# Threshold attention followed by a leaky-ReLU layer pair: head 2 masked on ScalarE in every step, turn copies moved to VectorE, and a rearranged start

## The chip, the cores and the metric

The kernel runs on one core of a Trainium2 chip. The metric is device time in microseconds (us), the median of several executions. The core has a matrix engine (TensorE, PE in the profile; PEld are its weight loads), a vector engine (VectorE, DVE), a scalar engine (ScalarE, ACT), GpSimd (POOL), and SyncE (SP), which here only issues transfers (DMAs).

## The reference

Eight batches, eight heads, 576 tokens, head size 64. The attention keeps only scores within `tau` = 0.02 of the row's maximum. Its output, with the heads side by side, is the input of two dense layers.

```python
scores = scale * np.matmul(q, k.transpose(0, 1, 3, 2))
thresh = np.max(scores, axis=-1, keepdims=True) - tau
scores = np.where(scores >= thresh, scores, -1000000000.0)
attn = np.exp(scores - np.max(scores, axis=-1, keepdims=True))
attn = attn / (np.sum(attn, axis=-1, keepdims=True) + 1e-09)
x = np.matmul(attn, v)            # then (B*S, H*D) = (4608, 512)
h = x @ w_in                      # 512 -> 2048
out = np.maximum(0.01 * h, h) @ w_out   # 2048 -> 512
```

## The kernel before, in words

**Steps.** The work is cut into 144 steps, 18 for each batch. A step handles 128 query rows of a pair of heads (head 1 and head 2 of the pair, `h` = 0 and 1 in the code) against all 576 keys; the last two steps of a batch (tail steps) take the last 64 tokens of two pairs each. Iteration `n` of the loop at the end of the function issues the scores of step `n` and the later stages of earlier steps. Every engine works through its own instructions strictly in the order in which this loop issues them; nothing reorders them.

**q and k** must be exact beyond fp16, so each fp32 block is split into a high and a low fp16 half, scaled by 64. For the first blocks this is done on ACT (high, L158) and DVE (low, L159) by `split_now`; for all others on POOL by `split_scale` (L138), `split_high` (L144) and `split_low` (L148). `turn` (L162) transposes both halves on PE (L177) into a PSUM tile `tp` and copies that to `qT` or `kT` (L188, for the tails L180). The `tp` tile shares a ring of two PSUM buffers (tag `h`) with `hp`, the result of layer 1. `turns_at` says in which iteration a block is turned: ten per batch, and those of the next batch fall on ten of its 18 iterations.

**Scores.** `scores` (L217) makes the three products high-high, low-high, high-low of both heads, 12 matmuls for a step, into two PSUM tiles (tag `sc`). `copy_min` (L225, DVE) scales and negates them into the SBUF tile `s` and yields the row minimum; it also frees the PSUM tiles for the next step. `threshold` (L232) adds `tau`; it runs on DVE for steps below 14 and on POOL from then on.

**Mask and exponential.** Two ways exist. In the plain way ACT computes `e = exp(min - s)` (L254) and DVE multiplies by the comparison with the threshold and sums (L264, `weights`). In the *steep* way, for head 2 only, ACT pushes everything beyond the threshold to a huge negative value with a Prelu of slope 1e20 (L250), which needs the threshold, and takes the exponential with its sum (L251). Head 1 always goes the plain way. A step is steep if its number is below 12, or if the iteration after it has no turn.

**Normalisation and product with v.** `recip` (L270, DVE) inverts the sums, `widen` (L273) writes them into the last block of the weights tile. That tile is then transposed. For `early` steps (below 8) PE transposes (L291) and ACT and DVE copy (L293, `turn_w_pe`); for the others `turn_w` is a DMA transpose on SP's queue (L281), and `widen` runs on POOL. `pv` (L304) multiplies with v, four iterations after the second step of a pair, three for early ones. `evacuate` (L326, L316 for tails, DVE) multiplies by the reciprocal and writes `x`.

**Layers.** `layer1` (L347) makes 16 matmuls per iteration into `hp`, and ACT applies the leaky ReLU (L349) into `g`. `layer2` (L360) makes eight matmuls per iteration into a single PSUM tile `o`; ACT copies it out (L366, `osb`) and SP stores it. After the last step the queues `l1q`, `l2q` and `stores` are drained in the same loop.

**The order at the start** is written out by hand: the first three blocks are split at once, turned, then pair 1's k block (`first[3]`) is split, then the loop begins. In iteration 0 pair 1's q block (`first[4]`) is split behind the first `copy_min` and ahead of `threshold`, and both blocks are turned at the end of that iteration.

```python
for st in steps:
    st.steep = st.n < 12 or not turns_at.get(st.n + 1)
```

Of the kernel before, what the change touches and what calls it, by code (L numbers as in the profile page):

```python
# [9 lines left out]
FP32 = mybir.dt.float32  # L10
# [4 lines left out]
PV_LAG = 4  # L15


class Group:


    def __init__(self, tokens, where):
        self.tokens = tokens
        self.where = where
        self.x = None
        self.g = None


class Step:


    def __init__(self, n, b, blk, p, c):
        self.n, self.b, self.blk, self.p, self.c = n, b, blk, p, c
        self.tail = blk == 2

        self.early = n < 8


@with_exitstack
def kernel(
# [10 lines left out]
    nc = tc.nc  # L50
# [9 lines left out]
    ps = ctx.enter_context(tc.tile_pool(name="ps", bufs=1, space=bass.MemoryType.PSUM))  # L60
# [3 lines left out]
    ident = sb.tile([128, 128], FP16, name="ident")  # L64
# [54 lines left out]
    def turned_of(b, which):  # L119
        if (b, which) not in turned:  # L120
            turned[b, which] = sb.tile([128, 2, NP, WIDE[which]], FP16, tag=f"{which}T", bufs=2, name=f"{which}T")
        return turned[b, which]

    def pair_of(b, p, which):
        return raws[b, p // 2, which][:, ds(2 * (p % 2), 2), :].rearrange("p h (t d) -> p h t d", d=64)

    def new_half():
        return sb.tile([128, 2, 4, 2, 64], FP16, tag="half", bufs=4, name="half")
# [12 lines left out]
    def split_high(key):  # L141
        n = 2 if key[1] == "t" else 4
        halves[key] = new_half()
        nc.gpsimd.tensor_copy(out=halves[key][:, 0, 0:n, :, :], in_=scaled[key][:, 0:n, :, :])  # L144
# [6 lines left out]
    def split_now(key):  # L151
        t = halves[key] = new_half()
        for i in range(2):
            if key[1] == "t":
                src, n = tails[key[0], key[2]][:, :, i, :], 2
            else:
                src, n = pair_of(*key)[:, i, :, :], 4
            nc.scalar.activation(out=t[:, 0, 0:n, i, :], in_=src, func=AF.Copy, bias=0.0, scale=64.0)  # L158
            nc.vector.scalar_tensor_tensor(out=t[:, 1, 0:n, i, :], in0=src, scalar=64.0, in1=t[:, 0, 0:n, i, :],  # L159
                                           op0=AX.mult, op1=AX.subtract)  # L160

    def turn(key, copy=None):  # L162
        copy = copy or nc.scalar.copy
        b, p, which = key
        dst, half = turned_of(b, which), halves.pop(key)
        n = 2 if p == "t" else 4
        c0 = 0 if which == "q" else 64
        if p == "t":
            c0 = MAIN if which == "q" else 0
            tp = ps.tile([128, 2, 2, 2, 64], FP16, tag="h", bufs=2, name="tp")  # L170
        else:
            tp = ps.tile([128, 2, 4, 128], FP16, tag="h", bufs=2, name="tp")
        for x in range(2):
            for t in range(n):
                for h in range(2):
                    o = tp[ds(64 * h, 64), x, :, t, :] if p == "t" else tp[ds(64 * h, 64), x, t, :]
                    nc.tensor.transpose(o, half[:, x, t, h, :], ident[:, :])  # L177
        if p == "t":
            for x in range(2):
                copy(out=dst[:, x, :, ds(c0, 64)], in_=tp[:, x, :, :, :].rearrange("d u s p -> d (u s) p"))  # L180
            if which == "k" and b:
                nc.gpsimd.tensor_copy(out=dst[:, :, :, 576:640], in_=dst[:, :, :, 0:64])
            elif which == "k":
                for x in range(2):
                    nc.vector.tensor_copy(out=dst[:, x, :, 576:640],
                                          in_=tp[:, x, :, :, :].rearrange("d u s p -> d (u s) p"))
        else:
            copy(out=dst[:, :, p, ds(c0, 512)], in_=tp[:, :, :, :].rearrange("d x t p -> d x (t p)"))  # L188
# [3 lines left out]
    steps = []  # L192
# [36 lines left out]
    def threshold(st):  # L229
        st.th = sb.tile([128, 2, 2], FP32, tag="th", bufs=3, name="th")  # L230
        eng = nc.vector if st.n < 14 else nc.gpsimd
        eng.tensor_scalar(out=st.th[:, :, 0], in0=st.mn[:, :, 0], scalar1=1.0, scalar2=tau_f, op0=AX.mult, op1=AX.add)  # L232
# [118 lines left out]
        if u == nu - 1:  # L351
            l2q.extend((g, m, r) for m in range(T // 128) for r in range(8))

    def layer2():
        g, m, r = l2q.pop(0)
        if r == 0:
            g.o = ps.tile([128, 512], FP32, tag="o", bufs=1, name="o")
        for j in (2 * r, 2 * r + 1):
            for u2 in range(2):
                nc.tensor.matmul(out=g.o[ds(64 * u2, 64), :], lhsT=g.g[:, j, ds(128 * m + 64 * u2, 64)],  # L360
                                 rhs=w_out16[:, j, :], start=(j == 0), stop=(j == 15), skip_group_check=True)
        if r == 7:
            nm = g.tokens // 128
            if m == 0:
                g.osb = sb.tile([128, nm, 512], FP32, tag=f"osb{nm}", bufs=2 if nm == 2 else 1, name="osb")
            nc.scalar.activation(out=g.osb[:, m, :], in_=g.o[:, :], func=AF.Copy, bias=0.0, scale=1.0)  # L366
            if m == nm - 1:
                stores.append(g)
# [13 lines left out]
    loads_at, turns_at, pool_at = {}, {}, {}  # L382

    def at(d, n, f):
        d.setdefault(n, []).append(f)

    def units(b):
        u = [(b, p, w_) for p in range(NP) for w_ in "kq"]
        return u[:2] + [(b, "t", "k")] + u[2:] + [(b, "t", "q")]

    for b in range(1, B):
        base = PERB * (b - 1)
        for i, (s, w_) in enumerate(((0, "k"), (0, "q"), (1, "k"), (1, "q"))):
            at(loads_at, base + ((-2, 0, 5, 7)[i] if b > 1 else (3, 4, 8, 9)[i]),
               lambda b=b, s=s, w_=w_: load_main(b, s, w_))
        for i, w_ in enumerate("kq"):
            at(loads_at, base + (2, 12)[i] + 4 * (b == 1), lambda b=b, w_=w_: load_tails(b, w_))
        for i, key in enumerate(units(b)):
            n_ = base + 4 + 18 * i // 10 if b > 1 else 9 + 3 * i // 2
            at(pool_at, n_ - 3, lambda key=key: split_scale(key))  # L400
            at(pool_at, n_ - 3, lambda key=key: split_high(key))
            at(pool_at, n_ - 2, lambda key=key: split_low(key))
            at(turns_at, n_, lambda key=key: turn(key))
    for b in range(B):
        base = PERB * (b - 1)
        if b:
# [46 lines left out]
    def split_pool(key):  # L453
        split_scale(key)
        split_high(key)
        split_low(key)

    first = units(0)
    for key in first[:3]:
        split_now(key)  # L460
    turn(first[0])
    turn(first[1], nc.vector.tensor_copy)
    turn(first[2])
    split_now(first[3])
    for key in first[5:7]:
        split_pool(key)
    for i in range(4):
# [1 line left out]
    for n_, key in zip((0, 1, 6), first[7:]):  # L469
        at(pool_at, n_, lambda key=key: split_pool(key))  # L470
    at(turns_at, 0, lambda: turn(first[3]))
    at(turns_at, 0, lambda: turn(first[4], nc.vector.tensor_copy))
    for n_, key in zip((1, 2, 3, 4, 8), first[5:]):
        at(turns_at, n_, lambda key=key: turn(key, nc.vector.tensor_copy if key[2] == "q" else None))

    N = len(steps)
    for st in steps:
        st.steep = st.n < 12 or not turns_at.get(st.n + 1)
    pv_at = {s.n + PV_LAG - s.early: s for s in steps if s.tail or s.c == 1}
    n = 0  # L480
    while n < N + PV_LAG + 2 or l1q or l2q or stores:
        for f in loads_at.get(n, []):
            f()
        if 1 <= n <= N:
            exps(steps[n - 1])
        if n < N:
            scores(steps[n])
            copy_min(steps[n])
        if n == 0:
            split_now(first[4])  # L490
        todo = pool_at.get(n, [])
        for f in todo[:1]:
            f()
        if n < N:
            threshold(steps[n])
        for f in todo[1:]:
            f()
        if 1 <= n <= N:
            last = steps[n - 1]
            weights(last)  # L500
            if last.early:
                recip(last.pair, last.c, 1)
                widen(last.pair, last.c, 1, nc.vector)
            elif last.tail or last.c == 1:
                recip(last.pair, 0, last.pair.n)
                widen(last.pair, 0, last.pair.n)
                turn_w(last.pair)
        while stores:
            store()
        if l1q and l1q[0][3] <= n:  # L510
            layer1()
        for f in turns_at.get(n, []):
            f()
        if 2 <= n < N + 2 and steps[n - 2].early:
            turn_w_pe(steps[n - 2].pair, steps[n - 2].c)
        for _ in range(2):
            if l2q:
                layer2()
        if n in pv_at:
            pv(pv_at[n])  # L520
            evacuate(pv_at[n], n)
        n += 1
# [33 lines left out]
```

## Time and profile before

| what | value |
|---|---|
| median of three runs | 517.52 us (516.12 to 518.38) |
| the profiled execution | 517.33 us |
| its span in the trace | 515.6 us |
| mean granted TensorE clock | 0.995 |
| POOL th (L232) waiting for DVE's minimum (L225), 50 to 480 us | 63.9 us, 70 times |
| ACT Prelu (L250) waiting for POOL's th, the same stretch | 3.2 us, 3 times |
| DVE weights (L264) | 210 instructions, mean 875 ns |
| ACT k and q copies (L188) | 60 instructions, 1008 ns |
| DVE q copies (L188) | 4 instructions, 688 ns |

The page names groups of instructions by source line, engine and tile. The rows of the timeline give a start, a length, the engine, the instruction and, in brackets, how long the engine had been idle before it and whose result ended the wait. In the chain of work that ended last, each row is a start and the time that this instruction adds to the chain, which can be less than its own length, since an engine begins its next instruction before the last one is quite through. A row in the table of windows has one column per engine with its busy time in that stretch.

### The profile page before, as it was taken

To read this page: it belongs to the slowest core of one execution; us is meant where nothing else is said; L and a number is where in the kernel's file an instruction comes from. 1 tells how busy PE (TensorE), PEld (TensorE's weight loads), DVE (VectorE), ACT (ScalarE), POOL (GpSimd) and SP (SyncE) were. 2 spreads that over 40 slices of the span, in tenths; PEclk is the share of its full clock that TensorE was granted. 3 is DMA by queue.
4 is the path that set the end of the run, shared out by engine and by line. 5 is a ranking of instruction groups with operands and counts; after the bars stand their busy time and mean duration, and the time that the engine had idled before them with its cause. 6 is when DMAs were issued, how large, how long until landed. Compare 5 with 4: busy or idle time off the path is not lost.

```text
span 515.6 us, 19350 instructions
## 1 busy us (share of the span) xinstructions
PE 482.9 (94%) x7904; PEld 343.9 (67%) x7904; DVE 432.6 (84%) x1208; ACT 431.8 (84%) x733; POOL 339.8 (66%) x537
## 2 busy tenths in 40 slices
PE   5676798899999999999999999999999999999995
PEld 3454576666677777777677777777677777666783
DVE  4899989899899889988899889988899888888200
ACT  4788977898899988998889888998889889999531
POOL 4990789877787777777787877777787873322000
PEclk9999999999999999999999999999999999999999
DMA  8993776999979879979979889979979988776711
GB/s 240 239 240 61 156 154 143 154 193 163 237 155 196 199 179 189 185 152 208 210 164 191 200 179 192 182 148 211 210 163 167 210 150 159 131 130 120 143 44 61
DMA packets 220697, 87.75 MB, mean 170 GB/s; under 512 B 190912, under 2 KB 217536, under 8 KB 220608
## 3 DMA queue, kind: packets, MB, share of 16 engines
q1 hardware_dynamic: 217648, 82.07, 77.9%
q0 software_dynamic: 2688, 4.19, 4.5%
q8 instruction: 61, 1.00, 0.8%
q10 hardware_dynamic: 272, 0.26, 0.1%
q14 instruction: 28, 0.23, 0.1%
HBM read 36.70 MB, written 9.44 MB: 89 GB/s over the span
## 4 chain that ended last, share of the span: by engine, by line
PE 72%; DVE 12%; DMA 6%; ACT 6%; issue 2%; POOL 1%; SPq 0%; DVEq 0%; POOLq 0%; ACTq 0%
PE hp L347 22%; PE o L360 21%; PE sc L217 18%; PE pv L304 6%; DMA wT<-w 6%; DVE s L225 5%; PE tp L177 4%; DVE w L264 4%; ACT e L254 2%; ACT s L250 1%; DMA rawt<-in_k_dram 1%; ACT w L251 1%; ACT g L349 1%; DVE th L232 1%; DVE wT L293 1%
## 5 line engine op out<-in xcount | busy, mean ns | idle before, releaser
L225 DVE TENSOR_SCALAR_CACHE_REDUCE s<-sc 128x576 f32<-128x576 f32 x288 | 206.1, 753 | 27.5 <-PE sc L217 24.8
L264 DVE SCALAR_TENSOR_TENSOR w<-s,th,e 128x576 f16<-128x576 f32 x210 | 178.9, 875 | 1.1 <-POOL th L232 0.8
L254 ACT ACTIVATE e<-s,mn 128x576 f16<-128x576 f32 x210 | 155.6, 773 | 1.7 <-DVE s L225 1.5
L360 PE MATMUL o<-wout,g 128*64 128x512 f16 x1152 | 147.8, 379 | 0.9 <-ACT osb L366 0.9
L217 PE MATMUL sc<-kT,qT 64*128 64x288 f16 (+1 forms) x1920 | 138.7, 288 | 9.9 <-DVE s L225 9.4
L347 PEld LDWEIGHTS <-win 128*64 128x64 f16 x2560 | 118.8, 110 | 35.0 <-issue 33.3
L347 PE MATMUL hp<-x,win 128*64 128x256 f16 x2048 | 137.8, 277 | 1.7 <-DVE x L326 1.7
L232 POOL TENSOR_SCALAR th<-mn 128x2 f32<-128x2 f32 x130 | 80.8, 622 | 88.1 <-DVE s L225 63.9
L349 ACT ACTIVATE g<-hp 128x512 f16<-128x512 f32 x144 | 85.0, 591 | 47.7 <-PE hp L347 46.6
L217 PEld LDWEIGHTS <-qT 64*128 64x128 f16 (+1 forms) x1920 | 78.2, 97 | 63.3 <-issue 48.9
L360 PEld LDWEIGHTS <-g 128*64 128x64 f16 x1152 | 62.8, 110 | 30.8 <-issue 1.6
L148 POOL TENSOR_TENSOR half<-scaled,half 128x512 f16<-128x512 f32 (+1 forms) x75 | 81.1, 1081 | 1.8
L250 ACT ACTIVATE s<-s,th 128x576 f32<-128x576 f32 x78 | 60.3, 773 | 5.0 <-POOL th L232 3.2
L251 ACT ACTIVATE w<-s,minus_tau 128x576 f16<-128x576 f32 x78 | 60.5, 775 | 4.3 <-DMA wT<-w 1.8
L177 PE MATMUL tp<-ident,half 128*64 128x128 f16 x1152 | 49.0, 227 | 10.5 <-ACT half L158 5.2
L304 PE MATMUL pv<-wT,v 128*64 128x256 f16 (+1 forms) x960 | 53.9, 247 | 3.5 <-DMA wT<-w 3.2
L304 PEld LDWEIGHTS <-v 128*64 128x64 f16 x960 | 43.2, 111 | 19.6 <-issue 5.3
L144 POOL CAST half<-scaled 128x512 f16<-128x512 f32 (+1 forms) x75 | 50.7, 676 | 7.6 <-PE tp L177 3.0
L138 POOL TENSOR_SCALAR scaled<-raw 128x512 f32<-128x512 f32 x60 | 48.0, 800 | 9.3 <-PE tp L177 6.1
L177 PEld LDWEIGHTS <-half 128*64 128x64 f16 x1152 | 42.0, 114 | 14.8 <-ACT half L158 5.8
L273 POOL CAST w<-rec 128x256 f16<-128x256 f32 (+1 forms) x76 | 29.1, 383 | 30.9 <-DVE rec L270 28.7
L188 ACT COPY kT<-tp 128x1024 f16<-128x1024 f16 x32 | 32.2, 1008 | 4.5 <-PE tp L177 4.5
(40 smaller groups left out, 277.2 us busy)
## 6 DMA issues: line engine op xcount, KB each, us to landing
vraw<-in_v_dram SPq DMA_DIRECT2D x16, 512.0 KB, 4.8
out_dram<-osb SPq DMA_DIRECT2D x16, 512.0 KB, 4.2
raw<-in_k_dram SPq DMA_DIRECT2D x14, 512.0 KB, 4.4
raw<-in_q_dram SPq DMA_DIRECT2D x14, 512.0 KB, 4.8
win<-in_moe_w_in_dram POOLq DMA_DIRECT2D x4, 512.0 KB, 9.8
wout<-in_moe_w_out_dram POOLq DMA_DIRECT2D x4, 512.0 KB, 13.1
wT<-w SPq DMA_TRANSPOSE x76, 5.5
raw<-in_k_dram SPq DMA_DIRECT2D x4, 256.0 KB, 4.7
```

Source lines behind the costliest of these rows:

```text
L148: nc.gpsimd.tensor_tensor(out=halves[key][:, 1, 0:n, :, :], in0=scaled.pop(key)[:, 0:n, :, :], in1=halves[key][:, 0, 0:n, :, :], op=AX.sub ...
L177: nc.tensor.transpose(o, half[:, x, t, h, :], ident[:, :])
L217: nc.tensor.matmul(out=o, lhsT=lhs, rhs=turned[st.b, "k"][rows, kx, pair, ds(key0, 288)], start=(i == 0), stop=(i == 2), skip_group_check= ...
L225: nc.vector.tensor_scalar(out=st.s[:, h, :].rearrange("p (a b) -> p a b", a=2), in0=st.sc[h][:, :, 0:288], scalar1=-1.0 / UNIT, scalar2=No ...
L232: eng.tensor_scalar(out=st.th[:, :, 0], in0=st.mn[:, :, 0], scalar1=1.0, scalar2=tau_f, op0=AX.mult, op1=AX.add)
L251: nc.scalar.activation(out=st.w[h], in_=z, func=AF.Exp, bias=minus_tau[:, :], scale=1.0, accum_out=st.sum[h])
L254: nc.scalar.activation(out=st.e[:, h, :], in_=st.s[:, h, :], func=AF.Exp, bias=st.mn[:, h, 0:1], scale=-1.0)
L264: nc.vector.scalar_tensor_tensor(out=st.w[h], in0=st.s[:, h, :], scalar=st.th[:, h, 0:1], in1=st.e[:, h, :], op0=AX.is_le, op1=AX.mult, ac ...
L304: nc.tensor.matmul(out=o, lhsT=v16[st.b % 2][:, st.p + u, blk, :], rhs=rhs, start=(i == 0), stop=(i == 4), skip_group_check=True)
L347: nc.tensor.matmul(out=hp[ds(64 * u2, 64), jj, :], lhsT=w_in16[:, i, ds(128 * j + 64 * u2, 64)], rhs=g.x[:, i, :], start=(i == 0), stop=(i ...
L349: nc.scalar.activation(out=g.g[:, ds(nj * u, nj), :], in_=hp[:, :, :], func=AF.Prelu, bias=0.0, scale=1.0, alpha=0.01)
L360: nc.tensor.matmul(out=g.o[ds(64 * u2, 64), :], lhsT=g.g[:, j, ds(128 * m + 64 * u2, 64)], rhs=w_out16[:, j, :], start=(j == 0), stop=(j = ...
```

## The change

- Every step is steep: head 2 is masked on ACT in all 144 steps, where it was 78.
- The copies behind the turns of batches 1 to 7, main and tail, q and k, go from ACT to DVE.
- At the start, the split of pair 1's k block moves behind the first scores and their minimum, and the threshold of step 0 behind that. The q block of pair 1 is turned in iteration 1 instead of 0, so behind the scores of step 1.
- `idle` issues products of the identity with itself, into the PSUM tile `pv`, whose result nobody reads: 34 before the first turn, 4 and 5 around the third, 16 in iteration 0 and 8 in each of the iterations 1 to 4. 91 in all.
- The weights of steps 6 and 7 are transposed by DMA instead of by PE (`early` is now `n < 6`); the iteration of their `pv` is unchanged.
- Behind the last step, layer 2 writes its sums into the two buffers that the scores no longer need, instead of the one tile `o`.

```diff
-        self.early = n < 8
+        self.early = n < 6
...
-    def layer2():
+    def layer2(n):
         g, m, r = l2q.pop(0)
-        if r == 0:
+        if r == 0 and n > N:
+
+            g.o = ps.tile([128, 2, 512], FP32, tag="sc", bufs=2, name="osc")[:, 0, :]
+        elif r == 0:
             g.o = ps.tile([128, 512], FP32, tag="o", bufs=1, name="o")
...
-            at(turns_at, n_, lambda key=key: turn(key))
+            at(turns_at, n_, lambda key=key: turn(key, nc.vector.tensor_copy))
...
+    def idle(n):
+
+        t = ps.tile([128, 4, 128], FP32, tag="pv", bufs=1, name="idle")
+        for i in range(n):
+            nc.tensor.matmul(out=t[:, 0, :], lhsT=ident[:, :], rhs=ident[:, :], start=True, stop=True,
+                             skip_group_check=True)
+
     first = units(0)
+    idle(34)
     for key in first[:3]:
         split_now(key)
     turn(first[0])
     turn(first[1], nc.vector.tensor_copy)
+    idle(4)
     turn(first[2])
-    split_now(first[3])
+    idle(5)
...
-    at(turns_at, 0, lambda: turn(first[4], nc.vector.tensor_copy))
+    at(turns_at, 1, lambda: turn(first[4], nc.vector.tensor_copy))
...
-        st.steep = st.n < 12 or not turns_at.get(st.n + 1)
-    pv_at = {s.n + PV_LAG - s.early: s for s in steps if s.tail or s.c == 1}
+        st.steep = True
+    pv_at = {s.n + PV_LAG - (s.n < 8): s for s in steps if s.tail or s.c == 1}
...
         if n == 0:
+            split_now(first[3])
+            threshold(steps[0])
             split_now(first[4])
+        if n < 5:
+            idle(8 if n else 16)
...
-        if n < N:
+        if 0 < n < N:
             threshold(steps[n])
...
-                layer2()
+                layer2(n)
```

## The prediction

> **What bounds the kernel now.** I read the page's head first, then the table of windows, then the chain of work that ended last, then the timeline where the first two disagreed with a PE-bound picture.
>
> ```profile
> span 515.6 us, 19350 instructions
> PE 482.9 (94%) x7904; PEld 343.9 (67%) x7904; DVE 432.6 (84%) x1208; ACT 431.8 (84%) x733; POOL 339.8 (66%) x537
> PE   5676798899999999999999999999999999999995
> ```
>
> PE is busy for 94% of the span, but not evenly: the first seven slices and the last are below 9. The windows (PE, PEld, DVE, ACT, POOL in that order, then granted clock) say what limits each stage:
>
> ```profile
> 0.00:10.00 10.00, 4.08 (x49) 2.79 (x51) 3.17 (x10) 5.26 (x13) 3.02 (x13) 1.00 0.71 224
> 20.00:30.00 10.00, 6.96 (x143) 5.20 (x139) 9.48 (x31) 8.94 (x16) 9.71 (x18) 1.00 1.07 238
> 30.00:40.00 10.00, 6.23 (x103) 4.11 (x98) 9.52 (x31) 8.26 (x16) 8.57 (x12) 1.00 1.20 231
> 60.00:100.00 40.00, 34.09 (x564) 24.61 (x565) 37.03 (x96) 31.81 (x51) 33.99 (x52) 0.96 0.76 147
> 150.00:200.00 50.00, 50.00 (x856) 35.46 (x856) 45.27 (x128) 45.05 (x75) 38.15 (x60) 1.00 0.88 183
> 450.00:475.00 25.00, 25.00 (x370) 17.00 (x366) 20.97 (x61) 24.09 (x46) 7.20 (x13) 1.00 0.72 130
> ```
>
> From 150 to 475 us PE does not idle: 50.00 of 50, 25.00 of 25. There nothing that DVE or ACT saves can shorten the span. Before about 80 us DVE is the bound (9.5 of 10) and PE idles. All PE work has to be done in any case, so the span is that work plus PE's idle time, 515.6 - 482.9 = 32.7 us, and a gain can only come out of that (and out of products that run slowly). The chain shows which DVE work sets the pace early on:
>
> ```profile
> 11.66 1.43 DVE s L225 x4
> 13.09 1.33 DVE half L159
> ...
> 44.87 0.18 DVE rec L270
> 45.07 0.23 DVE w L273
> 45.30 0.40 DVE qT L180 x2
> 45.70 0.40 DVE wT L293
> ```
>
> Each row is a start, the share of the chain and an instruction. One step's minima (L225) cost 1.36 to 1.45 us, one head's weights (L264) 0.74, rec 0.18, widen (L273) 0.24, a wT copy 0.40, a q copy on DVE 0.60 (0.68 by its own row), x 0.33. These are start-to-start prices, and I add with them.
>
> **The change, part by part.** Sums are against the profiled execution: 517.33 us, of which 515.6 are the span. The median shown is 517.52, 0.19 above it.
>
> *A. First scores ahead of pair 1's split, idle products.* Before, the first scores (PE, from 8.66) take 2.12 us for 12 products, against 0.91 for the same 12 later; the first 32 transposes take 2.29 us against 0.61 per 16 later. PE runs at half speed until about 18 us, though the clock column says 1.00. DVE starts the first minimum only at 11.66, because two lows of pair 1 (9.85 to 11.73) stand ahead of it. After: kT's copy at 7.05 stays, since ACT's tail split ahead of it waits for the rawt transfer (6.58). Tail transposes at warm speed end near 8.45 instead of 8.73, the DVE tail copies near 9.55 instead of 9.94, the scores near 10.1, and the first minimum starts near 10.2 instead of 11.66. The two lows of pair 1 now follow it (11.5 to 12.9), then th, the two lows of q (to 14.5), then min 1 at 14.5, before 17.02. Then th, weights, rec, widen, and the q copy, which the diff moves behind min 1: it ends near 17.9, the scores of step 2 take 0.9, min 2 starts near 18.9. Before it started at 20.66. I take **-1.8**. The 34 idle products have no row. They start when ident is there (1.30). Lower bound: 115 ns each, the pace of a pair of half-width transposes at the slow clock (15 in 0.86 us at 11.79): 3.9 us, done at 5.2, just when the first transposes can start. Upper bound: the weight load exposed as well (114 ns by row L177): 7.8 us, done at 9.1, which moves everything behind by up to 1.9 and eats the gain. I take the lower, because the weight loads of the other products are mostly covered. Range of A: -2.5 to +0.3. The other 57 idle products (about 0.9 us after step 0, 0.45 to 0.9 in iterations 1 to 4) lie in PE's idle time: PE reaches the q and w transposes there about 2 us before DVE wants them. Without that cover they would cost 3 us.
>
> *B. W of steps 6 and 7 by DMA.* DVE loses two rec, two widen and two wT copies (0.36 + 0.47 + 0.80) and gains one rec (0.18): **-1.45**, on the DVE chain. ACT loses two copies of 0.67 and PE 40 transposes, neither on the chain. New: the widening goes to POOL, which sat idle for 9.07 us before its widen at 51.74, and the transpose to SP's queue. The one at 52.16 took 3.20 us, the median is 5.5. From rec at about 44.9 the data lands at 48.8 to 51.0; pv of step 7 stood at 49.12 and DVE wants its result only at 51.59. So pv may wait up to 1.9 us in PE's queue, with the scores of step 11 behind it (needed by DVE at 51.90); I take 0, bounds 0 to +1.0. Queued behind the new transpose on SP is one load of q (second half, batch 1), first read by POOL at iteration 15: no cost.
>
> *C. Turn copies on DVE where head 2 was already masked on ACT.* Iterations 9, 10 and 12 had one weights instruction before and have one now; DVE gains two main copies and one pair of tail copies: 0.60 + 0.60 + 0.40 = **+1.6**, all in the stage that DVE bounds. ACT loses 0.90 + 0.90 + 0.64, hidden.
>
> *D. Iterations 13 to 19, where a turn meets two weights instructions.* Each of the five turns (13, 15, 16, 18, 19) loses a weights instruction on DVE and gains a copy: 0.74 - 0.60 = 0.14 if undisturbed. But these weights were stretched where POOL worked beside them:
>
> ```profile
> 59.49 1.25 DVE L264 SCALAR_TENSOR_TENSOR w<-s,th,e 128x576 f16<-128x576 f32 x1
> 60.67 1.15 DVE L264 SCALAR_TENSOR_TENSOR w<-s,th,e 128x576 f16<-128x576 f32 x1
> ...
> 62.89 0.28 PE L217 MATMUL sc<-kT,qT 64*128 64x288 f16 x1 [1.93 <-DVE s L225]
> 63.57 1.59 PE L217 MATMUL sc<-kT,qT 64*128 64x288 f16 x11 [0.40 <-DVE s L225]
> ```
>
> The pair takes 2.34 us here, 1.97 at 76.26, 2.4 at 79.95, and 1.5 to 1.6 in iterations 15 and 16. The q copy, by contrast, took 0.68 in all four instances, also at 30.96 beside a POOL cast. One weights plus one copy is 1.34: savings of 1.0 + 0.2 + 0.2 + 0.63 + 1.06 = 3.1 at most, 0.7 at least (the remaining weights may meet POOL instead). I take **-1.9**. The last two rows show the second effect: PE waits 1.93 and 0.40 us, and then 11 score products take 1.59 instead of 0.89 and layer 1 1.92 instead of 1.06, 1.5 us in all, in the chain. If DVE is a microsecond earlier, that stall shrinks; **-0.8** (0 to -1.6).
>
> The Trainium skill (TensorE: Matmul & The Clock Gate, "Part 1: The HAM clock gate") has the clock halve only after an idle window of about 3.4 us, which would make the 2.3 us of waiting here harmless. The row shows the halving, so the row decides; by the page alone the second term of D would be 0 and the forecast 0.8 higher.
>
> *E. Steps from 80 to 150 us.* PE idles there some 5.6 us, in waits of 0.5 to 1.1 for wT transfers, x, g. DVE gets lighter, ACT does not. I take **-0.3**, bounds -2 to +2.
>
> *F. 150 to 475 us.* Per batch a turn iteration on DVE goes from 1.36 + 1.48 to 1.36 + 0.74 + 0.60. On ACT it goes from e, e, g, copy (1.33 + 0.48 + 0.90 = 2.71) to e, s, w, g (0.67 + 0.80 + 0.77 + 0.48 = 2.72). PE needs 2.69 for the shortest iteration and 3.14 for one with a turn, so both stay under it: **0**.
>
> *G. The end.* In the drain, group sums of layer 2 alternate between two buffers; the last group waited 0.69 us for its predecessor's copy (row L360, 507.37). **-0.65**. Other hand-overs there are already hidden under layer 1.
>
> Sum: -1.8 - 1.45 + 1.6 - 1.9 - 0.8 - 0.3 + 0 - 0.65 = **-5.3**, so 517.33 - 5.3 = **512.0 us**.
>
> **Rivals.**
> 1. *The front gives back what it gains.* The idle products last to 9 us (A is 0), pv of step 7 waits (B is -0.45), the remaining weights meet POOL (D is -0.7, no cold stall saved): 0 - 0.45 + 1.6 - 0.7 + 0 - 0.65 = -0.2, giving 517.1. For it: POOL is 86 to 97% busy from 20 to 40 us. Against it: these are three separate mishaps. Anything up to half of them lands between 514.9 and 517.
> 2. *More goes than I count.* D at its limits (-3.1 - 1.6) and E at -2 give -1.8 - 1.45 + 1.6 - 4.7 - 2 - 0.65 = -9.0, 508.3. For it: PE's waits up to 150 us all name DVE, or a transfer behind POOL.
> 3. *Slower: ACT starts to wait for POOL's th.* In the 66 steps that had both heads multiplied on DVE, ACT needed only the minimum; now its Prelu (L250) needs th from POOL, and those are the iterations in which POOL splits. Behind the Prelu stand w and g, and g frees the buffer that layer 1 of the next iteration needs. In the trace ACT waited for th 3 times, at most 2.58 us (before the Prelu at 82.48). It decides from about 1.4 us: by the times of F, g could start 1.4 us later than layer 1 ends before PE feels it. If one in four of the 65 such steps after 60 us costs PE 0.9 us (the wait before layer 1 at 82.80), that is 16 times 0.9, +14.4, giving 526.4. Against it: POOL waits 63.9 us in total for DVE's minimum before th, so it is mostly early.
>
> **Chances.** Forecast (510 to 514.9) 0.50; more than counted (below 510) 0.22; front given back (514.9 to 520) 0.18; slower by rival 3 0.10. The predicted time is that of the likeliest, 512.0. The range leaves out about a tenth on each side: 508.0 to 517.5. A measurement of this kernel tells about 0.5% (2.6 us) from no change: below 514.9 is faster (0.72), above 520.1 slower (0.10), between them 0.18.
>
> **What would show it.** A: first transposes at about 0.6 us per 16, min 0 near 10.2, min 2 near 18.9. B: no wT copy for steps 6 and 7; pv of step 7 without a wait on wT. C and D: min 19 (78.29 before) near 74; no score row of 1.59 near 63. E: PE idle under 8 us from 40 to 100 (9.8 before). F: PE 50.00 of 50 in the windows from 150 on. G: the last 32 layer-2 products directly behind the 32 ahead of them. PE idling after 150 us with ACT waiting for th would make the forecast wrong, and so would a first minimum later than 11 us.

## The result, and the profile after

The changed kernel takes **521.1 us** (median of 20 runs, 517.78 to 524.56); the kernel before took 517.5 us beside it (20 runs, 515.8 to 518.83). The ratio is **1.0068 (95% interval 1.0048 to 1.0088)**, 3.5 us slower. The forecast was 512.0 us, the range 508.0 to 517.5: wrong in sign, and the time lies outside the range. The profiled execution of the changed kernel took 518.73 us, near the lower end of its runs.

The head of its page and the slices of the granted clock:

```profile
span 516.9 us, 19546 instructions
PE 489.2 (95%) x7955; PEld 348.2 (67%) x7955; DVE 419.4 (81%) x1155; ACT 433.8 (84%) x779; POOL 313.2 (61%) x538
...
PEclk9887799999999999999999999999999999999999
```

DVE has indeed lost work (432.6 to 419.4 us) and ACT gained none to speak of. PE is "busier" only because the 91 idle products count (8.6 us). The clock row is new: slices 2 to 5 are at 7 and 8 tenths. The table of windows (columns as in the prediction) shows where:

```profile
30.00:40.00 10.00, 7.48 (x89) 4.70 (x86) 9.52 (x28) 7.53 (x13) 7.69 (x10) 0.68 1.21 219
40.00:60.00 20.00, 16.02 (x190) 10.40 (x184) 17.39 (x51) 14.08 (x24) 6.16 (x10) 0.73 0.64 138
...
150.00:200.00 50.00, 49.84 (x860) 35.24 (x858) 43.76 (x119) 45.23 (x81) 32.78 (x58) 1.00 0.93 183
450.00:475.00 25.00, 25.00 (x362) 17.09 (x360) 20.42 (x58) 24.08 (x45) 6.59 (x12) 1.00 0.71 137
```

From 150 us on PE is as full as before, so the loss of this execution is made in the first 150 us. It is an execution 2.4 us quicker than the median of 521.1, and no profile of the changed kernel shows where the others lose that; longer executions of two kernels close to it show something (x1 and y1, below). To find the loss I set the start of every step's first minimum against the same step before. One such lead is good to about 1 us: kernels that keep the start of before begin step 0 in their profiles between 0.11 us later and 1.06 us earlier than it. The changed kernel leads by 1.84 us at step 0, by 0.68 at step 2, by 0.11 at step 4. It is 3.42 behind at step 13, 0.47 ahead again at step 22, **1.81 behind at step 23**, and 2.22 behind at the last step, 143. Between steps 22 and 23 alone it loses 2.28 us. It is back to 0.50 behind at step 36 and then loses 1.94 us between steps 39 and 40, where `pv` (at 149.00 us) waits 1.73 us for a transfer of weights.

The timeline of the changed kernel between steps 22 and 23 (start, length, engine, instruction, in brackets the idle time before it and what ended it):

```profile
89.19 1.06 PE L347 MATMUL hp<-x,win 128*64 128x256 f16 x16
...
89.75 1.16 POOL L148 TENSOR_TENSOR half<-scaled,half 128x512 f16<-128x512 f32 x1
...
90.08 0.39 PE L177 MATMUL tp<-ident,half 128*64 128x128 f16 x8
...
91.00 0.19 POOL L232 TENSOR_SCALAR th<-mn 128x2 f32<-128x2 f32 x1
91.22 0.77 ACT L250 ACTIVATE s<-s,th 128x576 f32<-128x576 f32 x1 [1.45 <-POOL th L232]
...
92.03 0.77 ACT L251 ACTIVATE w<-s,minus_tau 128x576 f16<-128x576 f32 x1
...
92.80 0.57 ACT L349 ACTIVATE g<-hp 128x512 f16<-128x512 f32 x1
...
93.43 0.64 PE L177 MATMUL tp<-ident,half 128*64 128x128 f16 x16 [2.95 <-ACT g L349]
```

and the same instructions of the kernel before:

```profile
90.05 0.60 ACT L349 ACTIVATE g<-hp 128x512 f16<-128x512 f32 x1
...
90.69 0.64 PE L177 MATMUL tp<-ident,half 128*64 128x128 f16 x16 [0.47 <-ACT g L349]
```

Read it from the bottom. Iteration 22 is, once layer 1 runs, the one iteration of the loop with two turns: the last of batch 1 (x8, the tails) and the first of batch 2 (x16). With `hp`, they want three buffers of the ring of two. So the second `tp` waits for `hp`'s buffer, which ACT's `g` frees. Before, `g` stood directly behind ACT's exponentials. Step 21 is steep now, so the Prelu and a second exponential stand ahead of `g`, and the Prelu waits 1.45 us for POOL's `th`, which is queued behind splits (it starts at 91.00 us, 3.8 us after its minimum was there). PE waits 2.95 us in place of 0.47.

### The profile page after: what moved, and what is told of

Same layout as the page of the kernel before. It is cut to its first block, busy times and chain, and to the rows that moved or that the text cites. A ratio compares the mean times of both kernels' runs of the same rounds, so it can differ in the third digit from the quotient of the medians.

```text
span 516.9 us, 19546 instructions
## 1 busy us (share of the span) xinstructions
PE 489.2 (95%) x7955; PEld 348.2 (67%) x7955; DVE 419.4 (81%) x1155; ACT 433.8 (84%) x779; POOL 313.2 (61%) x538
## 3 DMA queue, kind: packets, MB, share of 16 engines
q8 instruction: 62, 1.02, 0.8%
## 4 chain that ended last, share of the span: by engine, by line
PE 77%; DVE 9%; DMA 5%; ACT 4%; POOL 2%; issue 2%; DVEq 0%; POOLq 0%
PE hp L347 24%; PE sc L217 20%; PE o L363 19%; PE pv L304 7%; PE tp L177 5%; DVE s L225 4%; DMA wT<-w 4%; PE osc L363 3%; DVE w L264 2%; ACT s L250 1%; ACT w L251 1%; DMA raw<-in_k_dram 1%; POOL half L148 1%; ACT e L254 1%; DVE qT L188 1%
## 5 line engine op out<-in xcount | busy, mean ns | idle before, releaser
L232 POOL TENSOR_SCALAR th<-mn 128x2 f32<-128x2 f32 x130 | 77.1, 593 | 121.3 <-ACT g L349 67.7
L363 PE MATMUL o<-wout,g 128*64 128x512 f16 x992 | 127.9, 379 | 0.0
L264 DVE SCALAR_TENSOR_TENSOR w<-s,th,e 128x576 f16<-128x576 f32 x144 | 126.6, 879 | 0.4 <-POOL th L232 0.4
L250 ACT ACTIVATE s<-s,th 128x576 f32<-128x576 f32 x144 | 110.5, 767 | 11.1 <-POOL th L232 9.1
L251 ACT ACTIVATE w<-s,minus_tau 128x576 f16<-128x576 f32 x144 | 111.7, 775 | 5.4 <-DMA wT<-w 0.6
L254 ACT ACTIVATE e<-s,mn 128x576 f16<-128x576 f32 x144 | 110.2, 765 | 3.4 <-DVE s L225 3.2
L177 PE MATMUL tp<-ident,half 128*64 128x128 f16 x1152 | 47.4, 222 | 6.9 <-ACT g L349 3.5
L177 PEld LDWEIGHTS <-half 128*64 128x64 f16 x1152 | 40.8, 112 | 10.1 <-issue 5.6
L144 POOL CAST half<-scaled 128x512 f16<-128x512 f32 (+1 forms) x75 | 43.5, 580 | 4.6
L138 POOL TENSOR_SCALAR scaled<-raw 128x512 f32<-128x512 f32 x60 | 39.2, 653 | 10.1 <-DMA raw<-in_k_dram 6.9
L326 DVE TENSOR_TENSOR x<-pv,wT 128x256 f16<-128x256 f32 x64 | 26.8, 419 | 7.1 <-PE pv L304 6.0
## 6 DMA issues: line engine op xcount, KB each, us to landing
vraw<-in_v_dram SPq DMA_DIRECT2D x16, 512.0 KB, 5.0
out_dram<-osb SPq DMA_DIRECT2D x16, 512.0 KB, 3.9
raw<-in_k_dram SPq DMA_DIRECT2D x14, 512.0 KB, 4.9
raw<-in_q_dram SPq DMA_DIRECT2D x14, 512.0 KB, 4.4
win<-in_moe_w_in_dram POOLq DMA_DIRECT2D x4, 512.0 KB, 10.4
wout<-in_moe_w_out_dram POOLq DMA_DIRECT2D x4, 512.0 KB, 11.0
```

The lines of the kernel that those rows point to most:

```text
L250: nc.scalar.activation(out=z, in_=z, func=AF.Prelu, bias=st.th[:, h, 0:1], scale=-1.0, alpha=1e20)
L251: nc.scalar.activation(out=st.w[h], in_=z, func=AF.Exp, bias=minus_tau[:, :], scale=1.0, accum_out=st.sum[h])
L254: nc.scalar.activation(out=st.e[:, h, :], in_=st.s[:, h, :], func=AF.Exp, bias=st.mn[:, h, 0:1], scale=-1.0)
L264: nc.vector.scalar_tensor_tensor(out=st.w[h], in0=st.s[:, h, :], scalar=st.th[:, h, 0:1], in1=st.e[:, h, :], op0=AX.is_le, op1=AX.mult, ac ...
```

## The experiments

The theories, as they arose: *the DMA transposes of steps 6 and 7* do it alone; *POOL's late th* does it alone; *the idle products* do harm; *the parts interact*; *a late load of q* makes POOL late everywhere; and last, *the two turns of iteration 22*. Ratios are to the kernel before, with 95% intervals; 0.1% is 0.5 us. Every edit is to the changed kernel unless "before" is said.

### Which part is it

**x1_w_on_pe**

```diff
-        self.early = n < 6
+        self.early = n < 8
```

> The changed kernel with one part undone: W of steps 6 and 7 is transposed by PE again, as before the change. Theory T1 (the front: pv of step 7 waits for the transfer, PE idles and its clock halves from 47 to 57 us) expects 2.5 to 4.5 us less than the changed kernel's 521.1, so 516.6 to 518.6, no wait of PE on wT before 60 us, and a full granted clock from 40 to 60 us. Theory T2 (ACT's Prelu behind POOL's th costs the time, after 70 us) expects less than 1 us of change, 520 to 521.5.

1.0069 (1.0047 to 1.0091), 520.37 us: nothing regained. In its profile the loss between steps 22 and 23 is there again (2.28 us). The DMA transposes are not the cause.

**x2_th_on_dve**

```diff
-        eng = nc.vector if st.n < 14 else nc.gpsimd
+        eng = nc.vector
```

> The changed kernel with the threshold of every step on DVE instead of POOL from step 14 on. T2 expects ACT's waits for th (9.1 us) gone, no wait of PE for ACT's g near 93 us (3.0) and 2 to 4.5 us less than 521.1, so 516.6 to 519. T1 expects less than 1 us of change, or somewhat more time, since DVE gains 130 instructions of 0.17 us, hidden where PE is the bound: 520 to 522.

1.0062 (1.0043 to 1.0081). PE's waits from 60 to 480 us (total, count, longest) show why this neither proves nor clears POOL:

```profile
PE hp L347 <- DVE x L326: 3.5, 5, 1.2
...
PE tp L177 <- ACT g L349: 1.0, 1, 1.0
```

The wait for `g`, at the same second turn of iteration 22, fell from 2.95 to 1.0, and steps 22 to 23 no longer lose. So two turns without the late `th` cost PE 1.0 us there. But DVE pays for 130 more thresholds, and PE now waits for DVE's `x`. A wait was exchanged for another; as the whole cause, "POOL's late th" falls.

**x3_masks_alone** (before, with only the steep steps and the copies on DVE)

```diff
-        st.steep = st.n < 12 or not turns_at.get(st.n + 1)
+        st.steep = True
...
-            at(turns_at, n_, lambda key=key: turn(key))
+            at(turns_at, n_, lambda key=key: turn(key, nc.vector.tensor_copy))
```

> The kernel before with only the masks and copies changed: all steps steep, copies of the turns of batches 1 to 7 on DVE. T2 expects this part alone to be slower than 517.5 by 1 to 4 us, with waits of ACT for th of 6 us or more. T1 expects 515.5 to 517.5: terms C, D and E of the prediction add to about -1.4.

1.0018 (0.9998 to 1.0039), 517.30 us. The masks alone bring the wait (2.94 us before `tp` at 93.92, behind a Prelu that waited 1.44) and the loss between steps 22 and 23 (2.27 us): it belongs to this edit and to no other.

**x4_start_alone** (before, with the new order at the start and the 91 idle products)

```diff
+    idle(34)
...
-    split_now(first[3])
+    idle(5)
...
+            split_now(first[3])
+            threshold(steps[0])
```

> The kernel before with only the rearranged start: first scores ahead of pair 1's split, q of pair 1 turned in iteration 1, and all 91 idle products. The prediction's term A expects -1.8, 515.7. The changed kernel's trace has the lead of 1.82 us at the first minimum shrunk to 0.25 at the fourth, so the other reading expects -0.3 to +0.3: 517.2 to 517.8.

1.0021 (1.0004 to 1.0038): the new start does not gain 1.8 us, it costs about 1.

**y1_no_idle**

```diff
     def idle(n):
+        return
```

> The changed kernel without its 91 idle products, nothing else. Theory T3 (the idle products do harm or nothing: they delay PE's transposes and move POOL's and DVE's work into each other) expects 1 us or more below the changed kernel's 521.1, so 517 to 520. Theory T4 (they keep the clock up and help) expects the first scores to take about 2.1 us again, the first minimum near 11 us and a time at or above 521.1.

1.0118 (1.0092 to 1.0144), 523.70 us. Without the idle products the changed kernel is 0.5% slower still: they help, and the third theory falls.

**y2_no_start** (the start of before; masks, DMA transposes and end of the change)

```diff
-    idle(34)
...
+    split_now(first[3])
```

> The changed kernel with the start of before: old order of the first splits, scores and threshold, q of pair 1 turned in iteration 0, no idle products. Masks, copies, W of steps 6 and 7 by DMA and the alternating buffers at the end stay. T5 (the parts only hurt together: the earlier start moves POOL's splits onto DVE's work, and with all steps steep ACT then waits) expects 516.5 to 518, the masks alone less the end's 0.7. T6 (the parts' prices simply add) expects 521.1 less the start's 1.1, 520.

1.0056 (1.0039 to 1.0072).

**y3_end_alone** (before, with the two buffers for layer 2's last sums)

```diff
+        if r == 0 and n > N:
+            g.o = ps.tile([128, 2, 512], FP32, tag="sc", bufs=2, name="osc")[:, 0, :]
```

> The kernel before with only the alternating buffers for layer 2 behind the last step. The prediction's term G expects -0.65: ratio 0.9987, 516.1 against 516.72. The other reading, that the wait moves into the copy or the store behind it, expects no change.

0.9981 (0.9972 to 0.9991): a gain of 1.0 us.

**y4_order_no_idle** (x4 without idle products)

```diff
     def idle(n):
+        return
```

> The kernel before with only the new order at the start (first scores ahead of pair 1's split, q of pair 1 in iteration 1) and no idle products. T3 expects less than with them (517.96): 516 to 517.3. T4 expects more than 517.96, with the half clock until 18 us as before.

1.0029 (1.0015 to 1.0044): the new order by itself costs about 1.5 us. On the kernel before, then, the idle products make no difference that these runs can tell (1.0021 with them); they help in the changed kernel alone (y1).

Masks, start and end by themselves (x3, x4, y3) sum to +0.20%; the change costs 0.68%. The DMA transposes and an interaction are still to be placed.

### Is it a late load of q?

After 150 us some profiles (x1, y1, y2) show ACT waiting for `th` again. Two of these executions took 522.21 us (x1) and 524.46 us (y1). PE idles there too, and every wait of PE from 150 to 473 us has one name; x1:

```profile
PE pv L304 <- DMA wT<-w: 1.8, 4, 0.9
```

In y1 it is 2.5 us in 5 waits; in the profile of the kernel before PE waits for nothing in that stretch. For ACT's waits the timeline of x1 shows one origin:

```profile
206.79 1.11 POOL L138 TENSOR_SCALAR scaled<-raw 128x512 f32<-128x512 f32 x1 [2.48 <-DMA raw<-in_q_dram]
...
208.51 0.40 POOL L273 CAST w<-rec 128x256 f16<-128x256 f32 x1
...
210.35 0.78 ACT L250 ACTIVATE s<-s,th 128x576 f32<-128x576 f32 x1 [2.28 <-POOL th L232]
```

POOL waits for a load, and `widen` and `th` queue behind it. I therefore issued that load two iterations earlier.

**z1_q_load_early**

```diff
-            at(loads_at, base + ((-2, 0, 5, 7)[i] if b > 1 else (3, 4, 8, 9)[i]),
+            at(loads_at, base + ((-2, -2, 5, 7)[i] if b > 1 else (3, 4, 8, 9)[i]),
```

> The changed kernel with one line changed: from batch 2 on, the first q load of a batch is issued two iterations earlier, beside that of k. Theory T8 (that load arrives when POOL already wants it; POOL then delays th and the widening, and with every step steep ACT's Prelu, its g and so PE wait for th) expects 2 to 3 us less than the changed kernel's 521.1, so 518 to 519, no wait of POOL for q after 150 us and a narrower spread of its runs. T6 (the loss sits in the first 100 us, in cold clocks and collisions) expects less than 0.5 us of change.

1.0085 (1.0054 to 1.0115): no gain. In its profile (522.68 us) POOL waits for q no more, and ACT's waits for `th` after 150 us are down to 0.4 us, from 5.2 in x1. PE still waits 3.0 us from 150 to 473 us, all of it for transfers of weights ahead of `pv`. So what PE loses there in that execution is not owed to ACT's `th`.

**z2_before_q_load_early** (the same edit on y3)

> The kernel before with the alternating buffers at the end (measured alone at 516.28) and the same early q load. T8 expects little, since in the plain steps ACT does not need th: 515.5 to 516.3. If the load itself were the loss whatever the masks, it would gain the 2 to 3 us here too.

1.0014 (0.9997 to 1.0030), against 0.9981 for y3: the earlier load itself costs 0.3%. The theory falls, though the wait is real.

**z3_masks_q_load_turn** (y3, masks, early load, and the turn of the next section moved)

> The kernel before with the masks and copies, the alternating buffers at the end, the early q load, and the last q turn of batch 1 moved from iteration 22, where it meets the first turn of batch 2, to iteration 20 (its split and its load three iterations earlier). The start and W of steps 6 and 7 are as before. The trace shows PE waiting 3.0 us for ACT's g between these two turns once every step is steep, and 0.5 before. T8 with this wait expects the masks to stop costing: 514.5 to 516. T6 expects 516.3 plus 0.9, 517.2.

1.0011 (0.9996 to 1.0025). The same kernel without the early load (v2, below) stands at 0.9956.

**z4_all_q_load_turn** (the changed kernel, early load, turn moved)

> The changed kernel with the early q load and the moved q turn. T8 with the wait at iteration 22 expects 2 us less than the changed kernel with the early load alone, 516 to 517.5. T6 expects no difference between the two.

1.0032 (1.0014 to 1.0051), against 1.0085 for z1: with the load held, moving the turn gives 0.5% back.

### The two turns of iteration 22

**v1_turn_moved** (the last turn of batch 1 goes from iteration 22 to 20, with its split and its load ahead of it)

```diff
-            at(loads_at, base + (2, 12)[i] + 4 * (b == 1), lambda b=b, w_=w_: load_tails(b, w_))
+            at(loads_at, base + (2, 12)[i] + (4 - 3 * i) * (b == 1), lambda b=b, w_=w_: load_tails(b, w_))
...
-            n_ = base + 4 + 18 * i // 10 if b > 1 else 9 + 3 * i // 2
+            n_ = base + 4 + 18 * i // 10 if b > 1 else (9, 10, 12, 13, 15, 16, 18, 19, 21, 20)[i]
```

> The changed kernel with only the last q turn of batch 1 moved from iteration 22 to 20 (split and tail load three iterations earlier, early q load not taken). Theory T9 (two turns in iteration 22 need the buffer that ACT's g frees, and g is late once step 21 is steep) expects 2.5 to 3.3 us less than 521.1: 517.8 to 518.6. If the early load made the difference in the earlier pair, it expects 520 or more.

**0.9991 (0.9976 to 1.0006)**, 516.52 us: 0.77%, 4.0 us, come back, all of the loss. PE's waits from 60 to 150 us, first of the changed kernel:

```profile
PE tp L177 <- ACT g L349: 3.5, 2, 3.0
...
PE pv L304 <- DMA wT<-w: 2.1, 2, 1.7
```

then of v1, whose answer is these two rows:

```profile
PE pv L304 <- DMA wT<-w: 3.7, 2, 2.1
PE sc L217 <- DVE s L225: 2.7, 5, 1.4
```

The row of `tp` is gone. The Prelu's own waits from 60 to 480 us hardly changed; the changed kernel, then v1:

```profile
ACT s L250 <- POOL th L232: 9.1, 9, 2.0
```

```profile
ACT s L250 <- POOL th L232: 8.5, 10, 1.8
```

So 8.5 us of such waits can stand without PE waiting for `g` once. What cost time was the one wait with a second turn due behind it. Between steps 22 and 23, v1 gains 1.22 us where the changed kernel loses 2.28. v1 also moves that turn's split on POOL, so the `th` of step 21 comes earlier (87.86 us, against 91.00), and its Prelu does not wait; v1 alone does not part the two. With x2 it can be said that the wait of 2.95 us needs both: with both turns but `th` in time it was 1.02. How much of the 4.0 us is which, and why it is 4.0 here and 2.7 between z1 and z4, these runs do not tell.

**v2_masks_turn_moved** (y3, masks, turn moved; start and transposes as before)

> The kernel before with masks and copies, the alternating buffers at the end, and the moved turn. T9 expects 514.5 to 516.3: the masks then cost nothing, and the end gives its 1.0. Without T9, 517 to 518.

**0.9956 (0.9942 to 0.9970)**, 514.68 us: faster than the kernel before and, with w2, the fastest of the study.

**v3_before_turn_moved** (y3, turn moved, masks as before)

> The kernel before with the alternating buffers at the end and the moved turn, masks as before. T9 expects little against the same kernel without the moved turn (516.28), since PE waits only 0.5 us there: 515.5 to 516.3. A gain of 2 us or more here would mean that the pair of turns costs whatever the masks.

1.0021 (1.0001 to 1.0041). The moved turn is no gain by itself: against y3 it costs 0.4%, for a reason that I did not find. Against v3, the masks gain 0.65%, 3.4 us; against y3, masks and moved turn together gain 0.25%, 1.3 us. Moved turn and masks pay only together.

**v4_masks_w_dma_turn** (v2 with steps 6 and 7 by DMA)

> The kernel of the second run here plus W of steps 6 and 7 by DMA. The prediction's term B expects 1.45 less than that run. Theory T1 (pv of step 7 waits, PE's clock halves) expects 1 to 3 us more.

0.9987 (0.9971 to 1.0004): the DMA transposes cost 0.31%, 1.6 us, against v2. The start then costs nothing (v1 against v4).

**w1_turn_moved_w_on_pe** (v1 with `early` at `n < 8`, so v2 with the new start)

> The changed kernel with batch 1's last turn moved and the weights of steps 6 and 7 turned by PE again. It lacks only the DMA transposes against the changed kernel with that turn moved (0.9991), and it has only the new start and the idle products more than the kernel of the fastest run (0.9956). If the DMA transposes cost what they cost without the new start (0.3%, 1.6 us), it stands near 0.996 and the new start is worth nothing either way. If instead the new start costs by itself what it costs on the kernel before (0.2 to 0.3%), and the idle products beside it make good what the DMA transposes lose, it stands near 0.9985.

1.0015 (0.9998 to 1.0032), 517.08 us. Neither figure was met: without the DMA transposes the new start costs 0.6%, with them nothing, and given the new start the transposes cost nothing, rather the reverse. The two parts do not add. The profile does not show why: w1 leads v2 by 0.9 us at step 54 and is level with it within 0.2 us at step 143. Part of that execution's loss came after that, by one transfer; `pv` of the last step waited as follows, against 0.18 us in v2:

```profile
481.70 0.74 PE L304 MATMUL pv<-wT,v 128*64 128x256 f16 x10 [1.31 <-DMA wT<-w]
```

**w2_idle_at_10_16** (v2 with idle products in the iterations 10 to 15)

```diff
+        if 10 <= n < 16:
+            idle(8)
```

> The kernel of the fastest run (all steps masked on ACT, turn moved, start of before), plus 8 products of the identity with itself at the end of each of the iterations 10 to 15, into the PSUM tile that layer 2 does not use yet. If the clock halves near 33 and 63 us because PE had too little to do, the half-pace stretch near 63 us goes and the kernel gains 0.5 to 1.5 us (0.994 or below, against 0.9956 without them). If waiting PE time costs nothing there because DVE sets the pace, it stays at 0.9956; if the 48 products get in the way of scores that DVE waits for, it loses up to 2 us (0.9995).

0.9952 (0.9937 to 0.9967), 514.86 us. In the profiled execution the edit did what it should; v2 in the edited iterations:

```profile
60.00:70.00 10.00, 8.23 (x124) 6.26 (x121) 8.22 (x21) 7.41 (x14) 7.66 (x12) 0.83 0.90 175
```

and w2, where the granted clock is full:

```profile
60.00:70.00 10.00, 9.08 (x163) 7.05 (x161) 9.09 (x23) 8.33 (x16) 7.75 (x12) 1.00 0.88 164
```

(From 30 to 40 us the clock is 0.83 in v2 and full in w2 as well, without an edit near it.) The median stayed: 0.04% between intervals of 0.15% each side. That does not show the half-pace stretches to be worth nothing. The profiled execution, 513.58 us, has a mean clock of 0.998; the other five of w2 lie at 0.990 to 0.995, where the ten of v2 lie (0.989 to 0.995), so by their clocks most of them still ran such stretches (one of 3.4 us takes 0.003 off the mean). In the profiled one steps 13 to 20 gained 2.93 us on the kernel before, against 1.34 in v2; but another execution of w2 took 513.61 us at a clock of 0.992. What a stretch is worth stays open.

## Why the prediction was wrong, by its own steps

**The step that failed is E, and with it rival 3.** The wait stands at 93 us, in E's stretch. E took -0.3 for it all, because "DVE gets lighter, ACT does not". It named PE's waits for `g` and did not ask what every step being steep puts into ACT's queue ahead of `g`; in the changed kernel that cost 2.28 us in one place. ACT's work was counted in F alone, for an iteration with *one* turn (2.72 us of 3.14). Rival 3 named the mechanism as it happened: the Prelu waits for `th`, `g` stands behind it and frees a buffer. But it took the buffer to be wanted only by layer 1 of the next iteration, 1.4 us later, and spread the price over 16 steps. The `tp` tiles share the ring, and where two turns fall in one iteration the second needs that buffer at once, with no slack. The row of before already showed it: PE waiting 0.47 us for `g` ahead of a `tp`, once in the stretch. Rival 2's sentence that PE's waits up to 150 us all name DVE, or a transfer, passes over that row. Shown by x3 (the masks alone bring the wait), by x2 (with `th` in time it is 1.02 us) and by v1 (without the second turn it is gone, and 0.77% with it). Rival 3's 526.4 us was too much: of the other waits for `th` none made PE wait for `g` longer than 0.5 us.

**F, 0 forecast.** In the profiled execution it held (49.84, then 50.00 of 50). In the profiled executions of x1, y1 and z1 (522.21, 524.46 and 522.68 us) it did not: PE waits 1.8, 2.5 and 3.0 us between 150 and 473 us for transfers of weights, for which F has no term. The profile of x3 has no such wait, so the masks alone need not bring them; what does is open.

**A, -1.8 forecast, about +1.1 measured** (x4, 0.21%; 0.12% between y2 and the change; 0 between v4 and v1, and 0.6% between v2 and w1). The first step came as told: 9.81 us against 10.2. The lead was then lost in two steps. The rows of DVE and PE in the changed kernel:

```profile
9.81 0.76 DVE L225 TENSOR_SCALAR_CACHE_REDUCE s<-sc 128x576 f32<-128x576 f32 x1 [0.42 <-PE sc L217]
...
11.18 2.01 DVE L159 SCALAR_TENSOR_TENSOR half<-raw,half 128x256 f16<-128x256 f32 x2
...
19.04 0.91 PE L217 MATMUL sc<-kT,qT 64*128 64x288 f16 x12 [1.54 <-DVE qT L188]
...
19.98 0.76 DVE L225 TENSOR_SCALAR_CACHE_REDUCE s<-sc 128x576 f32<-128x576 f32 x1 [1.00 <-PE sc L217]
```

The lows of pair 1 took 2.01 us beside POOL's casts where I counted 1.4, so minimum 2 starts at 19.98, not 18.9. The rest I had not priced at all: I carried the lead of step 2 through to the end, but from 20 to 45 us DVE's instructions are stretched where POOL works beside them. Summed over that stretch, what DVE's instructions took beyond the median of their kind (over these three profiles) is 0.34 us before, 2.38 in the changed kernel and 1.66 in x4. The lead lost between steps 2 and 6 goes with it: 1.7 us in the changed kernel, 1.4 in x4, and 0.7 in v1, which has the same start as the changed kernel and an excess of 0.86. So what the start saved, the bound stage behind it took back, by an amount that differs from one execution to the next. x4's own loss comes later in its profile: it is 0.03 us ahead at step 19 and 1.88 behind at step 21, after `pv` waited 2.50 us for a transfer of weights. The idle products behaved by my lower bound (34 in 3.81 us from 1.36 us on).

**B, -1.45 forecast; +1.6 measured without the new start** (v4 against v2), about 0 with it (x1 against the change). In the profile of the changed kernel the step that failed is "I take 0" for the wait of `pv`. I also left out that the 40 transposes which PE lost had kept it busy; no run shows what that is worth. The timeline of the changed kernel:

```profile
46.35 3.18 SPq L281 DMA_TRANSPOSE wT<-w  x1
...
51.43 1.28 PE L304 MATMUL pv<-wT,v 128*64 128x256 f16 x10 [1.29 <-DMA wT<-w]
...
52.64 1.62 PE L217 MATMUL sc<-kT,qT 64*128 64x288 f16 x12
...
54.19 1.92 PE L347 MATMUL hp<-x,win 128*64 128x256 f16 x16
```

The transfer takes 5.04 us in the chain, past the late end of my estimate (data at 51.4, estimated 48.8 to 51.0). PE waits 1.29, and `pv`, scores and layer 1 behind it all run at half pace. The lead goes from 0.28 at step 9 to 3.42 behind at step 13, and most of that is regained by step 20. Of these 3.70 us only some 2 are B's: x3 and v2, without the DMA transposes, lose 1.64 and 1.65 there, which is C. The 1.6 us of v4 are not in this stage: its profile leads that of v2 by 1.30 us at step 22 and by 2.08 at step 54, more than B's 1.45. It is 0.18 behind at step 143 and 1.7 at the end of the span. Part of what lies between are waits of `pv` for transfers of weights, 1.09 us at 364 us and 1.25 at the last step (v2: 0.18 at most after 150 us). Why such transfers come late is open, as in F.

**C, D and E, together -1.4** (+1.6 - 1.9 - 0.8 - 0.3): alone +0.9 (x3), since they bring the wait of iteration 22. With that turn moved, -3.4 against v3, whose own 0.4% is not explained, and -1.3 against y3. So once the wait is away the direction was right; which size is right is open. By the profiles of x3 and v2, steps 8 to 12 lose 1.3 us (C, +1.6 forecast) and steps 13 to 20 gain 1.2 and 1.3 (D, -2.7 forecast). The last term of D, -0.8 for the half clock, is not settled: in w2's profiled execution, at full clock, steps 13 to 20 gained 2.93. Step 19 started at 79.38, not near 74, and PE's idle time from 40 to 100 us was 10.1 us, not under 8.

**G, -0.65 forecast, -1.0 measured** (y3). The last 64 products run without a gap:

```profile
504.98 7.07 PE L363 MATMUL osc<-wout,g 128*64 128x512 f16 x64
```

**What stays open:** the parts that I measured (-1.0, +0.9 and +1.1 alone, +1.6 on top of v2) sum to +2.6 us of the 3.5; the rest lies within their intervals. The interaction of start and DMA transposes (v1, v2, v4, w1) is measured and not explained, and the runs of the changed kernel spread over 6.8 us, more than any of these terms. The transfers of weights that come late after 150 us are seen in several profiles, most of all in the longer executions (x1, y1, z1), and no run tests them.

## What to carry to other kernels

When an edit lengthens an engine's queue ahead of an instruction that frees a buffer, list every user of that buffer's ring in every iteration, and look for the one iteration in which two of them meet: by the prediction's estimate the average iteration had 1.4 us to spare; that one had none. A wait costs by what is queued behind it and due, not by its length: of nine waits of ACT for `th`, 9.1 us in all, one made PE wait long for `g`. A profile is one execution: look where in the spread of the runs it lies before taking it for the median. Time won at the start counts only if no bound stage follows that can take it back.

## What the runs showed of the hardware

- Ahead of the last products, PE's half-pace stretches are all 3.4 us long or a multiple of it (3.4, 6.8 and 10.2 in the changed kernel, from 13.1, 33.6 and 47.3 us). They follow lightly loaded time, not only full idleness: the one at 47.3 us began after waits of 1.13 us and less. By the timeline PE was busy for 1.67, 1.44 and 1.76 us of the 3.4 us ahead of the three, and for 3.22, 3.26 and 2.83 of the 3.4 us before those, which ran at full clock. The Trainium skill (TensorE: Matmul & The Clock Gate, "Part 1: The HAM clock gate") has a window of about 3.4 us; the lengths agree with it, the need for a whole idle window does not show here.
- Near the start the clock column reads 1.00 while the first 12 scores take 2.12 us, against 0.91 later; with idle products ahead of them they took 1.29.
- A multiply of two SBUF operands on DVE (L264) took 0.81 us undisturbed, 1.25 at 47.86 us and 1.79 at 33.90 us with POOL at work beside it; the q copy from PSUM stayed at 0.66 to 0.69.
